# Layer 2 of six of nine token blocks in pairs, with seven block products in place of eight

## The chip, the core and the metric

The kernel runs on one core of one Trainium2 chip. The metric is device time in microseconds (us) of one execution. TensorE (PE) multiplies, VectorE (DVE) and ScalarE (ACT) work elementwise, GpSimd (POOL) and SyncE (SP) issue DMAs. Each engine takes its instructions strictly in its own order and waits on semaphores for the others.

## The reference, cut to what matters

An attention with pooled keys feeds two feed-forward layers of the same shape. A token block is 512 rows; there are nine.

```python
attn_out = _attn_ref(q, k, v)                  # 8 heads of 64: x is 4608 x 512
h = x @ w_in                                   # layer 1: 512 -> 2048
g = P(h) / (Q(h) + 1e-6)                       # rational function, elementwise
x = g @ w_out                                  # 2048 -> 512
h = np.maximum(x @ w_in2, 0.0)                 # layer 2: 512 -> 2048
out = h * h @ w_out2                           # 2048 -> 512
```

## The kernel before

Every fp32 operand of a large product is held as two parts, HI (rounded to fp32r) and LO (the rest), and each product is three passes: HI*HI, HI*LO, LO*HI. The hidden width of 2048 is cut into 16 tiles of 128. A **slot** is one hidden tile of one token block: `mm1` makes h in one PSUM bank with 12 matmuls of 512 columns (4 row blocks times 3 passes), ACT and DVE turn h into g (`first`, `second`), and three slots later (LAG) `mm2` adds the tile's part of the output into four PSUM banks y0 to y3, again with 12 matmuls. So a slot is 24 matmuls, and 9 blocks, 2 layers and 16 tiles make 288 slots.

The blocks go in groups (SBS: 2, 2, 2 and 3 blocks). A group runs four phases of 8 tiles: two for layer 1, two for layer 2. A phase's eight weight tiles (1 MB each: w_in and w_out rows, HI and LO) stay in eight buffers `w` while all blocks of the group use them; after the first group they come from a copy in DRAM, `ws`. After a phase, ACT or DVE take the four banks out to `ya`, `yb` or `t` (`evac`). The attention of later blocks (36 chunks of 128 tokens) lies between the slots, as do the decoding of the weights in the first group and the DMA transposes and pooled sums of the attention.

The order on each engine is not the order of the code. The code records operations with costs, and the class `Plan` lists them on each engine by due time; `Plan.emit` writes them out in that order. All compute is recorded in helper functions, so the profile gives one line (L390) for nearly every row, and rows are told apart by tile names: `h<-x,w` is mm1, `y<-w,g` mm2 of layer 1 or `y<-g,w` the other operand order, `sc`, `xp`, `e`, `mx`, `q`, `a`, `at` belong to the attention, `kp`, `vp` to the pooled sums.

Of the kernel before, what the change touches and what calls it, by code (L numbers as in the profile page):

```python
# [22 lines left out]
POOL = 8  # L23
# [16 lines left out]
SBS = [[0, 1], [2, 3], [4, 5], [6, 7, 8]]  # L40
# [6 lines left out]
NORM_DVE = {0, 2, 3, 5}  # L47
# [5 lines left out]
TWOS = {c for sb in SBS for c in range(max(NF, CPB * sb[0]), CPB * sb[-1] + CPB - 1, 2)}  # L53
# [5 lines left out]
X_DMA = ()  # L59
SB1_START, SB1_STEP = 39, 3  # L60
# [51 lines left out]
class PlannedTile(View):  # L112
    def __init__(self, pool, bufs, shape, dtype, name):
        super().__init__(self)
        self.pool, self.bufs, self.shape, self.dtype, self.name = pool, bufs, shape, dtype, name
        self.writes, self.reads, self.made, self.psum = [], [], None, False

    def real_tile(self):
        if self.made is None:
            self.made = self.pool.tile(self.shape, self.dtype, name=self.name)  # L120
        return self.made
# [9 lines left out]
class Plan:  # L131
# [15 lines left out]
    def tile(self, pool, bufs, shape, dtype, name):  # L147
        t = PlannedTile(pool, bufs, shape, dtype, name)
        tiles = self.tags.setdefault((id(pool), name), [])
        tiles.append(t)  # L150
        return t
# [245 lines left out]
def fused_kernel(  # L397
# [13 lines left out]
    out: bass.AP,  # L411
):
# [3 lines left out]
    class Pool:  # L416
# [4 lines left out]
        def tile(self, shape, dtype, name):  # L421
            t = plan.tile(self.pool, self.bufs, shape, dtype, name)
            t.psum = self.psum
            return t
# [5 lines left out]
    px = Pool("px", 4)  # L430
    pw = Pool("pw", FH)
    PS = bass.MemoryType.PSUM
    ps_h = Pool("ps_h", 2, space=PS)
# [4 lines left out]
    scratch = {}  # L438
    sb_of = {j: sb for sb in SBS for j in sb}

# [38 lines left out]


# [34 lines left out]
    wt, raw_t = {}, {}  # L515
# [15 lines left out]

    def w_decode(ph, f):
# [13 lines left out]
        t = pw.tile([128, 2, 2 * TB], F32R, "w")  # L546
# [10 lines left out]
        wt[f] = t  # L557
# [29 lines left out]
    def kv_first():  # L587


        k, v = (px.tile([128, 2, 4, TB], F32, "x").rearrange("p a b c -> p (a b c)") for _ in range(2))  # L590
        kr = k[:, 0:H // 2 * S].rearrange("p (g k r) -> p g k r", g=H // 2, r=POOL)
        vr = [v[0:min(128, S - 128 * c), TB * c:TB * (c + 1)] for c in range(5)]
        for b, t in enumerate((k, v)):
            kp_t[b] = t[:, 6 * TB:6 * TB + H // 2 * SP].rearrange("p (g k) -> p g k", g=H // 2)
            vp_t[b] = t[0:SP, 7 * TB:8 * TB]

        def k_sum(b):
            plan.ahead = K_AHEAD if b == 0 else 0.0
            for g in range(H // 2):
                load(128 * S * 4, kr[:, g], kf[b, g].rearrange("p (k r) -> p k r", r=POOL))  # L600
                dve(S, "tensor_reduce", out=kp_t[b][:, g], in_=kr[:, g], axis=AX.X, op=ALU.add)
# [4 lines left out]
        def v_sum(b):  # L606
            plan.ahead = AHEAD if b == 0 else 0.0
            ps = ps_h.tile([128, TB], F32, "h")[0:SP]
# [43 lines left out]
    def q_first(c):  # L652

        if c == 0:
            t = f32(pw.tile([128, 2, 2 * TB], F32R, "w")).rearrange("p a n -> p (a n)")
            q_in[0] = t.rearrange("p (c h t) -> p c h t", c=4, h=4)
# [189 lines left out]
    def x_out(c):  # L846
        ps = x_ps.pop(c)
        j, o = divmod(c, CPB)
        if o == 0:
            xt[j] = px.tile([128, 2, 4, TB], F32R, "x")  # L850
        x = xt[j][:, :, :, o * CH:(o + 1) * CH]
        sc = 2.0 ** -A_SHIFT / POOL
        act(TB, AF.Copy, out=x[:, HI], in_=ps, scale=sc)
        stt(TB, x[:, LO], ps, sc, f32(x[:, HI]), ALU.mult, ALU.subtract)
# [6 lines left out]
    def mm1(i, u, f):  # L861
        ps = ps_h.tile([128, TB], F32, "h")
        w, x = wt[f], xt[u[0]]
        started[i] = pe(2.72, [
            dict(
                out=ps, lhsT=w[:, a, kc * 128:(kc + 1) * 128], rhs=x[:, b, kc, :],
# [6 lines left out]
    def mm2(i, u, f, ds=range(4)):  # L873
        g, w = gt[i], wt[f][:, :, TB:2 * TB]
        if f == 0:
            yps[u] = [ps_y.tile([128, TB], F32, f"y{d}") for d in range(4)]
        for d in ds:
            dd = slice(d * 128, (d + 1) * 128)
            mm = []
            for n, (a, b) in enumerate(PASSES):  # L880
                l, r = (w[:, a, dd], g[:, b]) if u[1] < 2 else (g[:, a, dd], w[:, b])
                mm.append(dict(
                    out=yps[u][d], lhsT=l, rhs=r,
                    start=(f == 0 and n == 0), stop=(f == FH - 1 and n == 2),
                ))
            pe(0.68, mm)

    def last_block(u, tiles):


        t, _ = ysb.pop(u[0])
        for d in range(4):
            for i in tiles:
                mm2(i, u, i % FH, (d,))
            for h in range(2):
                hh = slice(h * TB // 2, (h + 1) * TB // 2)
                tt(TB // 2, t[d][:, hh], yps[u][d][:, hh], t[d][:, hh], ALU.add)
                r0 = u[0] * TB + d * 128
                load(2 ** 17, out[r0:r0 + 128, hh], t[d][:, hh])

    def evac(u):
        j, ph = u
        y = yps.pop(u)
        if ph % 2 == 0:
            k = sb_of[j].index(j)
            if k < 2:
                t = p1.tile([128, 4, TB], F32, "y" + "ab"[k])
                ysb[j] = [t[:, d] for d in range(4)], t
            else:
                t = [p2.tile([128, 2, H, CH], BF16, "t") for _ in range(2)]  # L910
                ysb[j] = [f32(t[d // 2].rearrange("p a h t -> p a (h t)")[:, d % 2]) for d in range(4)], None
            for d in range(4):
                act(TB, AF.Copy, out=ysb[j][0][d], in_=y[d])
            return
        t, whole = ysb.pop(j)
        for d in range(4):
            tt(TB, t[d], y[d], t[d], ALU.add)
            if ph == 1:
                act(TB, AF.Copy, out=xt[j][:, HI, d], in_=t[d])
                if j in X_DMA:  # L920
                    act(TB, AF.Copy, out=xt[j][:, LO, d], in_=t[d], scale=-1.0)
            else:
                r0 = j * TB + d * 128
                load(2 ** 18, out[r0:r0 + 128, :], t[d])
        if ph == 1 and j in X_DMA:
            load_add(2 ** 20, f32(xt[j][:, LO]), whole)
        elif ph == 1:
            for d in range(4):
                tt(TB, xt[j][:, LO, d], t[d], f32(xt[j][:, HI, d]), ALU.subtract)

    def first(i, u):

        h = hps[i]
        s = p2.tile([128, TB], F32, "s")
        if u[1] >= 2:
# [3 lines left out]
        v = p2.tile([128, TB], F32, "v")  # L939
        t = p2.tile([128, TB], F32, "p")  # L940
# [8 lines left out]
        mid[i] = (s, v, t)  # L949

    def second(i, u):
        hps.pop(i)
        w = p1.tile([128, TB], F32, "w")
        g = p3.tile([128, 2, TB], F32R, "g")
        gt[i] = g
        if u[1] >= 2:
            (r,) = mid.pop(i)
            act(TB, AF.Square, out=g[:, HI], in_=r)
# [3 lines left out]
        q, r0, p = mid.pop(i)  # L962
# [7 lines left out]
    units = []  # L970
    for sb in SBS:
        for ph in range(4):
            units += [(j, ph) for j in sb]
    N = len(units) * FH
    nxt = {}
    for n, u in enumerate(units[:-1]):
        if units[n + 1][1] != u[1]:
            nxt[u] = units[n + 1][1]


# [147 lines left out]
```

## Time and profile before

| what | value |
|---|---|
| three runs | 1687.99, 1689.12, 1690.29 us, median 1689.12 |
| profiled execution | span 1686.5 us from first to last instruction; the profile gives no time of its own beside the span |
| PE busy | 1664.1 us, 99% |
| VectorE, ScalarE busy | 1126.8 us (67%), 1110.3 us (66%) |
| DMA | 237.8 MB, q1 (SP) busy 39.4% of 16 engines, q0 (POOL) 7.9% |

The median lies 2.6 us above the profiled span: start and end of an execution that the span leaves out. A share of busy time is a mean over stages; the windows in the rows below tell them apart. Matmuls are pipelined: one row of a matmul of 512 columns reads 389 ns, but the next begins long before that, so the pace is read from the starts of groups.

### The profile page before, as it was taken

Reading aid. Unit: us, or ns where it says so; the run is one execution under the profiler, and the core shown is the slowest. Engines: PE = TensorE matmul, PEld = TensorE weight load, DVE = VectorE, ACT = ScalarE, POOL = GpSimd, SP = SyncE. Lnnn points to the kernel's source line nnn. Section 1 sums busy time; section 2 is a strip of 40 time slices with the busy share of each in tenths; the row PEclk is TensorE's granted clock in tenths of the full one; section 3 lists DMA queues with packets and bytes.
Section 4 is the critical chain, followed back from the end, with each engine's and each line's share of the span. In section 5 each row is a group of like instructions: output and inputs, shape, how many; then the busy total and the mean of one; then the engine's idle time right before and its main releaser. Section 6 shows DMA issues by size and latency. Waiting matters only on the chain.

```text
span 1686.5 us, 23265 instructions
## 1 busy us (share of the span) xinstructions
PE 1664.1 (99%) x8764; PEld 1362.6 (81%) x8764; DVE 1126.8 (67%) x1794; ACT 1110.3 (66%) x2260; POOL 77.6 (5%) x95
## 2 busy tenths in 40 slices
PE   7899999999999999999999999999999999999998
PEld 4687888888888888888888888888888888888887
DVE  7999996664888963344899953447988998111112
ACT  6989778896566767765666877667766665333332
POOL 0001100110000111100001111000000000000000
PEclk9999999999999999999999999999999999999999
DMA  8358678978523565836145767646104005004001
GB/s 276 111 206 234 175 242 274 257 204 253 173 100 127 130 200 118 228 76 200 49 164 133 188 169 158 176 125 188 26 26 175 1 1 200 1 1 175 25 26 50
DMA packets 106976, 237.81 MB, mean 141 GB/s; under 512 B 63632, under 2 KB 65520, under 8 KB 86384
## 3 DMA queue, kind: packets, MB, share of 16 engines
q1 hardware_dynamic: 96352, 216.17, 39.4%
q0 software_dynamic: 10512, 20.16, 7.9%
q8 instruction: 69, 1.13, 0.3%
q14 instruction: 43, 0.35, 0.1%
HBM read 176.69 MB, written 42.99 MB: 130 GB/s over the span
## 4 chain that ended last, share of the span: by engine, by line
PE 92%; DVE 5%; ACT 2%; DMA 1%; issue 0%; SPq 0%; DVEq 0%; ACTq 0%
PE h L390 44%; PE y L390 44%; PE xp L390 2%; PE sc L390 1%; DVE w L390 1%; DVE p L390 1%; DVE g L390 1%; ACT v L390 1%; DMA ya<-wa 0%; DVE s L390 0%; ACT w L390 0%; ACT yb L390 0%; DVE t L390 0%; DMA w<-qf 0%; DVE x L390 0%
## 5 line engine op out<-in xcount | busy, mean ns | idle before, releaser
L390 PE MATMUL h<-x,w 128*128 128x512 f32 x3456 | 834.8, 390 | 3.7 <-DVE p L390 3.4
L390 PEld LDWEIGHTS h<-x,w 128*128 128x128 f32 x3456 | 645.9, 188 | 141.7 <-DVE p L390 3.0
L390 PE MATMUL y<-g,w 128*128 128x512 f32 x1728 | 418.0, 390 | 0.7 <-DVE g L390 0.7
L390 PE MATMUL y<-w,g 128*128 128x512 f32 x1728 | 417.2, 390 | 0.0
L390 PEld LDWEIGHTS y<-g,w 128*128 128x128 f32 x1728 | 323.2, 188 | 68.4 <-DVE g L390 1.2
L390 PEld LDWEIGHTS y<-w,g 128*128 128x128 f32 x1728 | 323.1, 188 | 67.6 <-DVE g L390 0.4
L390 DVE TENSOR_TENSOR g<-w,g 128x512 fp32r<-128x512 f32 x144 | 99.5, 691 | 314.9 <-ACT g L390 305.8
L390 ACT ACTIVATE s<-h 128x512 f32<-128x512 f32 x288 | 171.7, 596 | 209.2 <-PE h L390 193.1
L390 ACT ACTIVATE v<-s,ln_bias 128x512 f32<-128x512 f32 x144 | 104.6, 726 | 145.4 <-DVE s L390 144.7
L390 ACT ACTIVATE g<-s 128x512 fp32r<-128x512 f32 x144 | 91.0, 632 | 95.2 <-PE y L390 94.8
L390 ACT ACTIVATE p<-h,a_sb 128x512 f32<-128x512 f32 x144 | 111.9, 777 | 42.7 <-PE h L390 41.2
L390 DVE SCALAR_TENSOR_TENSOR g<-p,a_sb,v 128x512 fp32r<-128x512 f32 x144 | 107.7, 748 | 29.0 <-ACT v L390 26.4
L390 DVE TENSOR_TENSOR p<-p,h 128x512 f32<-128x512 f32 x144 | 98.0, 680 | 21.5 <-ACT p L390 9.4
L390 DVE SCALAR_TENSOR_TENSOR w<-p,a_sb,w 128x512 f32<-128x512 f32 x144 | 107.5, 747 | 2.0
L390 DVE SCALAR_TENSOR_TENSOR p<-p,a_sb,h 128x512 f32<-128x512 f32 x144 | 106.6, 740 | 2.0 <-ACT v L390 0.8
L390 DVE SCALAR_TENSOR_TENSOR s<-s,b_abs,v 128x512 f32<-128x512 f32 x144 | 107.1, 744 | 0.0
L390 ACT ACTIVATE v<-h,b_sb 128x512 f32<-128x512 f32 x144 | 99.3, 690 | 10.2 <-DVE p L390 5.6
L390 ACT ACTIVATE v<-v,ex_bias 128x512 f32<-128x512 f32 x144 | 104.1, 723 | 2.8
L390 DVE SCALAR_TENSOR_TENSOR w<-s,g 128x512 f32<-128x512 f32 x144 | 99.1, 688 | 3.3
L390 DVE TENSOR_TENSOR g<-w,v 128x512 fp32r<-128x512 f32 x144 | 98.7, 685 | 1.5
L390 ACT ACTIVATE w<-s 128x512 f32<-128x512 f32 x144 | 91.0, 632 | 9.6 <-DVE g L390 6.8
L390 ACT ACTIVATE e<-e,sm 128x72 f32<-128x72 f32 x256 | 69.9, 349 | 1.4 <-DVE sm L390 1.1
(111 smaller groups left out, 1058.0 us busy)
## 6 DMA issues: line engine op xcount, KB each, us to landing
w<-ws SPq DMA_DIRECT2D x96, 1024.0 KB, 5.5
ws<-w SPq DMA_DIRECT2D x32, 1024.0 KB, 5.5
q<-qt SPq DMA_DIRECT2D x27, 512.0 KB, 3.8
kp<-kt POOLq DMA_DIRECT2D x42, 288.0 KB, 4.6
wraw<-wb SPq DMA_DIRECT2D x8, 1024.0 KB, 7.2
wraw<-wa SPq DMA_DIRECT2D x7, 1024.0 KB, 6.4
yb<-wa SPq DMA_DIRECT2D x6, 1024.0 KB
vp<-vt POOLq DMA_DIRECT2D x42, 144.0 KB, 4.1
```

What stands on the lines that cost most here:

```text
L390: made = fn(**{k: v.real() if isinstance(v, View) else v for k, v in kw.items()})
```

## The change

Blocks 0 and 1 keep the four phases. Blocks 2 to 8 then run layer 1 one block at a time over all 16 tiles (`("one", j)`), with the weight tiles fetched again for each block. Block 2 runs layer 2 in the old way (`("two", 2)`). Blocks 3 and 4, 5 and 6, 7 and 8 run layer 2 as **pairs**. In a pair the two halves of each operand make 2 x 2 block matrices: the two token blocks are the columns on one side, and w_in and w_out are cut in two on both sides. Strassen's scheme (the form with shared sums) takes seven block products p1 to p7 where eight stood. A block product is a **group** of 6 matmuls of 512 columns; a pair has 8 double tiles times 7 groups for h, and 4 rounds times 7 products times 2 halves for y: 112 groups.

The operands of the products are sums of the halves. Those of the weights (`w_sums`, 8 double tiles times two parts) are made once on DVE and ACT and stored in DRAM (`wf`); those of the token blocks (`pair_forms`, tiles `xf`) are made at the start of a pair; those of g (`prepare`, tiles `gf`) at each round. The sums of products are not made on PE alone: a group is added on top of the bank of an earlier one (chains p1, p6, p7, p4 in one bank and p5, p3 in another), and after each group ACT or DVE read the partial sum out of the open bank into `ga`, `gb`, `gc`, `gd` (for h) or `acc` (for y). The next group in that bank waits for this read.

The weight loads of a pair are 72 pieces of 0.25 or 0.5 MB (`wi`, `wo`). The x of blocks 3 to 8 goes to DRAM when its attention is done (`xd`, 256 KB pieces with rows of 512 bytes) and comes back before the block. All chunks from 8 on scale their attention weights on DVE (`NORM_DVE`). The last half-tile evacuation (`last_block`) is gone. Results of the pairs are stored transposed.

The core of the diff:

```diff
-SBS = [[0, 1], [2, 3], [4, 5], [6, 7, 8]]
+FIRST_TWO = [0, 1]
+PLAIN = 3
+PAIRS = [(3, 4), (5, 6), (7, 8)]
+SEQ = [
+    ("one", 2), ("one", 3), ("two", 2), ("one", 4), ("pair", (3, 4)), ("one", 5), ("one", 6),
+    ("pair", (5, 6)), ("one", 7), ("one", 8), ("pair", (7, 8)),
+]
+PAIR_SLOTS, PAIR_STEPS = 28, 4
+NFT = DFF // 128
...
+NORM_DVE = {0, 2, 3, 5} | set(range(8, NCHUNK))
...
+SUM_AT = {n: 49 + 4 * (n - 4) for n in range(4, 8)} | {n: 98 + 2 * n for n in range(4)}
+CHUNK_AT = (
+    {8 + n: 38 + 3 * n for n in range(8)} | {16 + n: 92 + 3 * n for n in range(6)}
+    | {22 + n: 128 + 4 * n for n in range(6)} | {28 + n: 190 + 3 * n for n in range(8)}
+)
...
+        s2, s1, s3, s4 = (s[:, i // 2, i % 2 * h:(i % 2 + 1) * h] for i in S_PLACES[part])
+        tt(h, s1, a21, a22, ALU.add)
+        tt(h, s2, s1, a11, ALU.subtract)
+        tt(h, s3, a11, a21, ALU.subtract)
+        tt(h, s4, a12, s2, ALU.subtract)
+        flat = s.rearrange("p a c -> p (a c)")
+        hi, lo = (o[:, i].rearrange("p a c -> p (a c)") for i in (HI, LO))
+        act(2 * TB, AF.Copy, out=hi, in_=flat)
+        tt(2 * TB, lo, flat, f32(hi), ALU.subtract)
+        sums_of[n, part] = pd.tile([128, 2, 4, h], F32, f"wf{n}_{part}")
+        load(WB, sums_of[n, part], f32(o), STORE_EARLY)
...
+    def pair_forms(pair):
+        a, b = pair
+        (b11, b21), (b12, b22) = x2.pop(a), x2.pop(b)
+        made = {}
+
+        def form(p, x):
+            t = x_tile([128, 2, 2, TB], "xf", FORM_TAGS[pair][p])
+            split(t[:, HI], t[:, LO], x, 2 * TB)
+            made[p] = t
+
+        n = 2 * TB
+        form("p1", b11)
+        form("p2", b21)
+        tt(n, b11, b12, b11, ALU.subtract)
+        form("p5", b11)
+        tt(n, b12, b22, b12, ALU.subtract)
+        form("p3", b22)
+        tt(n, b22, b22, b11, ALU.subtract)
+        form("p6", b22)
+        form("p7", b12)
+        tt(n, b21, b21, b22, ALU.subtract)
+        form("p4", b21)
+        forms[pair] = made
...
+    Y_FORMS = (("p1", "p2"), ("p5", "p3"), ("p6", "p7"), ("p4",))
+    Y_ORDER = [p for ps in Y_FORMS for p in ps]
+    H_ORDER = ("p1", "p2", "p6", "p5", "p7", "p3", "p4")
+    HEAD_ORDER = ("p1", "p2", "p5", "p6", "p3", "p7", "p4")
...
+        def wi(n):
+            t = w_tile([128, 2, 4 * HT], "wi", 6 * (n % 2))
+            load(WB / 2, f32(t[:, :, 0:TB]), src(n, 0, slice(0, TB)), FETCH_EARLY)
+            load(WB / 2, f32(t[:, :, TB:2 * TB]), sums(n, 0, 0), FETCH_EARLY)
+            u = w_tile([128, 2, 4 * HT], "wi", 6 * (n % 2) + 1)
+            load(WB / 2, f32(u[:, :, 0:TB]), sums(n, 0, 2), FETCH_EARLY)
+            load(WB / 4, f32(u[:, :, TB:TB + HT]), src(n, 1, slice(HT, TB)), FETCH_EARLY)
+            at = {p: (t, m) for m, p in enumerate(FIRST_H)} | {p: (u, m) for m, p in enumerate(LAST_H)}
+            return {p: t[:, :, m * HT:(m + 1) * HT] for p, (t, m) in at.items()}
...
+            def step(p):
+                if not w:
+                    w.update(wi(n))
+                a, b, c, d = (t[:, q] for t in blocks_of(r))
+                if p == "p1":
+                    bank["x"] = ps_h.tile([128, TB], F32, "h", f"h{n if n < 2 else 0}")
+                if p in ("p2", "p5"):
+                    bank["z"] = ps_y.tile([128, TB], F32, "hz", "y3" if n == 1 else "y0")
+                x = bank["z" if p in ("p2", "p5", "p3") else "x"]
+                op = pe(1.36, [
+                    dict(
+                        out=x, lhsT=w[p][:, i, kt * 128:(kt + 1) * 128], rhs=forms[pair][p][:, j, kt],
+                        start=(p in ("p1", "p2", "p5") and m == kt == 0), stop=(m == 2 and kt == 1),
+                        skip_group_check=True,
+                    )
+                    for m, (i, j) in enumerate(PASSES) for kt in range(2)
+                ])
+                t = dict(p1=a, p2=a, p6=b, p5=d, p7=d, p3=b, p4=c)[p]
+                if p in ("p1", "p5", "p6"):
+                    act(TB, AF.Copy, out=t, in_=x)
+                elif p == "p4":
+                    sq(t, x)
+                else:
+                    tt(TB, t, x, t, ALU.add)
+                    sq(t, t)
+                return op
+
+            return [lambda p=p: step(p) for p in (HEAD_ORDER if n < 2 else H_ORDER)]
...
+            def prepare(k):
+                p = Y_ORDER[k]
+                a, b, c, d = blocks_of(r)
+                n = 2 * TB
+                if p == "p5":
+                    tt(n, a, b, a, ALU.subtract)
+                elif p == "p6":
+                    tt(n, d, d, a, ALU.subtract)
+                elif p == "p4":
+                    tt(n, c, c, d, ALU.subtract)
+                x = dict(p1=a, p2=c, p5=a, p3=d, p6=d, p7=b, p4=c)[p]
+                t = p1.tile([128, 2, 2, TB], F32R, "gf", "y" + "ab"[k % 2])
+                split(t[:, HI], t[:, LO], x, n)
+                if p == "p3":
+                    tt(n, b, d, b, ALU.subtract)
+                ring[p] = t
+                if k % 2 == 0:
+                    ws.update(wo(r, k // 2))
+
+            def group(k, i):
+                p = Y_ORDER[k]
+                if i == 0:
+                    prepare(k)
+                if not acc:
+                    acc.extend(f32(w_tile([128, 4, TB], "acc", 4 + m)) for m in range(2))
+                if p == "p1":
+                    bank["x", i] = ps_y.tile([128, TB], F32, "yx", f"y{1 + i}")
+                if p in ("p2", "p5"):
+                    bank["z", i] = (ps_h if i else ps_y).tile([128, TB], F32, "yz", "h1" if i else "y3")
+                x = bank["z" if p in ("p2", "p5", "p3") else "x", i]
+                op = pe(1.36, [
+                    dict(
+                        out=x, lhsT=ws[p, q][:, a, i * 128:(i + 1) * 128], rhs=ring[p][:, b, q],
+                        start=(p in ("p1", "p2", "p5") and m == q == 0), stop=(m == 2 and q == 1),
+                        skip_group_check=True,
+                    )
+                    for m, (a, b) in enumerate(PASSES) for q in range(2)
+                ])
+                o = dict(p1=0, p2=0, p6=1, p3=1, p4=2, p5=3, p7=3)[p]
+                t = acc[i][:, o]
+                if r == 0 and p in ("p1", "p5", "p3", "p4"):
+                    act(TB, AF.Copy, out=t, in_=x)
+                else:
+                    tt(TB, t, x, t, ALU.add)
+                if r == FH // 2 - 1 and p in ("p2", "p6", "p7", "p4"):
+                    r0 = (2 * (o // 2) + i) * 128
+                    load(2 ** 18, outt[(ta, tb)[o % 2], r0:r0 + 128, :], t)
+                return op
+
+            return [lambda k=k, i=i: group(k, i) for k in range(7) for i in range(2)]
...
+        hs = [h_steps(n) for n in range(FH)]
+        steps = [h for two in zip(hs[0], hs[1]) for h in two]
+        for r in range(1, FH // 2):
+            for h, y in zip(hs[2 * r] + hs[2 * r + 1], y_steps(r - 1)):
+                steps += [h, y]
+        return steps + y_steps(FH // 2 - 1)
```

The engine orders show it at three places. First PE near the end of layer 2 of block 8 (h the hidden tile, y0 to y3 the output banks). Before:

```order
L390 MATMUL h_14954<-x_11370,w_14288 128x512 x12
L390 MATMUL y0_14934<-w_14185,g_14891 128x512 x3
L390 MATMUL y1_14940<-w_14185,g_14891 128x512 x3
L390 MATMUL y2_14946<-w_14185,g_14891 128x512 x3
L390 MATMUL y3_14950<-w_14185,g_14891 128x512 x3
L390 MATMUL h_14986<-x_11370,w_14327 128x512 x12
```

And in the last pair now (h and hz are the two banks of a hidden double tile, yx and yz those of y, two of each):

```order
L409 MATMUL h_14691<-xf_14049,wi_14493 128x512 x6
L409 MATMUL hz_14751<-xf_13993,wi_14493 128x512 x6
L409 MATMUL yz_14761<-gf_14675,wo_14655 128x512 x6
L409 MATMUL h_14691<-xf_14023,wi_14553 128x512 x6
L409 MATMUL yz_14782<-gf_14746,wo_14687 128x512 x6
L409 MATMUL hz_14751<-xf_14012,wi_14553 128x512 x6
L409 MATMUL yz_14800<-gf_14746,wo_14687 128x512 x6
L409 MATMUL h_14691<-xf_14067,wi_14553 128x512 x6
L409 MATMUL yz_14782<-gf_14776,wo_14687 128x512 x6
L409 MATMUL yz_14800<-gf_14776,wo_14687 128x512 x6
```

A bank such as h_14691 now comes back every three or four groups with other work between, where before it held one sum of 12 matmuls and was read once.

Second, DVE at the end of the program (t is the output tile before; acc the output, gf the LO part of a form of g, ga to gd its sums). Before:

```order
L390 TENSOR_TENSOR g<-w,g 128x512 x6
L390 TENSOR_TENSOR t<-y_14934,t 128x256 x2
L390 TENSOR_TENSOR t<-y_14940,t 128x256 x2
L390 TENSOR_TENSOR t<-y_14946,t 128x256 x2
L390 TENSOR_TENSOR t<-y_14950,t 128x256 x2
```

And now, the first twelve rows from the last hidden sum on (eight more of the same kinds follow):

```order
L409 TENSOR_TENSOR gb<-hz,gb 128x512
L409 TENSOR_TENSOR gf<-gc,gf 128x1024
L409 TENSOR_TENSOR acc<-yx,acc 128x512
L409 TENSOR_TENSOR ga<-gb,ga 128x1024
L409 TENSOR_TENSOR acc<-yx,acc 128x512
L409 TENSOR_TENSOR acc<-yz,acc 128x512
L409 TENSOR_TENSOR gb<-gd,gb 128x1024
L409 TENSOR_TENSOR gf<-ga,gf 128x1024
L409 TENSOR_TENSOR acc<-yz,acc 128x512
L409 TENSOR_TENSOR gf<-gd,gf 128x1024
L409 TENSOR_TENSOR gd<-gd,ga 128x1024
L409 TENSOR_TENSOR acc<-yz,acc 128x512
```

PE's own end is now `yx<-gf,wo` x12, `yz<-gf,wo` x36 and `yx<-gf,wo` x36, 14 groups with no h group between them, and each product needs a form from this list.

Third, the SP queue in layer 2. Before, one of the 1 MB fetches for each slot:

```order
L390 DMA w<-ws_0_3473 128x2048
L390 DMA w<-ws_1_3588 128x2048
L390 DMA w<-ws_2_3631 128x2048
L390 DMA w<-ws_3_3796 128x2048
L390 DMA w<-ws_4_3872 128x2048
```

And in the last pair now:

```order
L409 DMA wo_14411<-wf2_1_6390 128x2x512
L409 DMA wo_14411<-wf3_1_6547 128x2x512
L409 DMA wi_14423<-wf5_0_3835 128x2x512
L409 DMA wi_14423<-ws3_3_3515 128x2x256
L409 DMA wi_14493<-ws3_4_3520 128x2x512
L409 DMA wi_14493<-wf6_0_4081 128x2x512
L409 DMA wo_14505<-wf2_1_6390 128x2x512
L409 DMA wo_14505<-wf3_1_6547 128x2x512
```

The same stretch of PE work is now fed by two to four pieces where one transfer stood.

## Rows read from the trace of the kernel before

**Rows 1.** Page: span and busy time of PE.

```profile
span 1686.5 us, 23265 instructions
...
PE 1664.1 (99%) x8764; PEld 1362.6 (81%) x8764; DVE 1126.8 (67%) x1794; ACT 1110.3 (66%) x2260; POOL 77.6 (5%) x95
```

**Rows 2.** Windows: us, busy of PE, PEld, DVE, ACT, POOL; granted clock; DMA.

```profile
0.00:40.00 40.00, 28.61 (x180) 17.06 (x180) 29.89 (x60) 23.52 (x69) 1.25 (x8) 0.91 0.85 289
40.00:80.00 40.00, 35.40 (x261) 27.44 (x260) 39.90 (x71) 38.85 (x94) 0.00 (x0) 1.00 0.34 119
...
200.00:300.00 100.00, 99.99 (x471) 82.06 (x470) 82.18 (x122) 78.29 (x145) 7.24 (x8) 1.00 0.76 238
300.00:400.00 100.00, 100.00 (x661) 81.99 (x660) 65.81 (x104) 85.94 (x215) 8.92 (x10) 1.00 0.82 221
...
1300.00:1400.00 100.00, 100.00 (x443) 82.84 (x442) 92.34 (x141) 62.66 (x99) 0.00 (x0) 1.00 0.08 29
...
1500.00:1600.00 100.00, 100.00 (x443) 82.83 (x442) 13.18 (x19) 38.03 (x63) 0.00 (x0) 1.00 0.24 84
```

**Rows 3.** All waits of PE: waiting engine and tile, releaser, us, times, longest.

```profile
PE y L390 <- DMA w<-qf: 8.0, 1, 8.0
PE h L390 <- DVE p L390: 3.4, 3, 1.6
```

**Rows 4.** Timeline of layer 2, last group: start us, length us, engine, tile.

```profile
1502.50 2.88 PE L390 MATMUL y<-w,g 128*128 128x512 f32 x12
1502.70 0.60 ACT L390 ACTIVATE s<-h 128x512 f32<-128x512 f32 x1 [2.09 <-PE h L390]
...
1505.22 2.88 PE L390 MATMUL h<-x,w 128*128 128x512 f32 x12
1505.42 0.63 ACT L390 ACTIVATE g<-s 128x512 fp32r<-128x512 f32 x1 [1.46 <-PE y L390]
1506.08 0.69 DVE L390 TENSOR_TENSOR g<-w,g 128x512 fp32r<-128x512 f32 x1 [4.75 <-ACT g L390]
```

**Rows 5.** Costliest groups by form: total busy us, mean ns of one.

```profile
L390 DVE TENSOR_TENSOR w<-wraw,w 128x1024 fp32r<-128x1024 f32 x12 | 14.6, 1221 | 4.2 <-ACT w L390 4.2
...
L390 ACT ACTIVATE w<-wraw 128x1024 fp32r<-128x1024 f32 x12 | 13.9, 1156 | 2.7 <-DVE wraw L390 1.8 <-PE y L390 0.9
```

**Rows 6.** Timeline of DVE in layer 1, back to back.

```profile
174.26 0.68 DVE L390 TENSOR_TENSOR p<-p,h 128x512 f32<-128x512 f32 x1
174.85 1.22 DVE L390 TENSOR_TENSOR w<-wraw,w 128x1024 fp32r<-128x1024 f32 x1
175.99 0.69 DVE L390 SCALAR_TENSOR_TENSOR w<-s,g 128x512 f32<-128x512 f32 x1
```

**Rows 7.** Timeline of the end.

```profile
1675.67 6.51 PE L390 MATMUL y<-w,g 128*128 128x512 f32 x28
...
1679.31 4.52 SPq L390 DMA_DIRECT2D out_dram<-t  x8
1681.54 1.43 DVE L390 TENSOR_TENSOR t<-y,t 128x256 f32<-128x256 f32 x4 [1.28 <-PE y L390]
```

**Rows 8.** Landing of the eight 256 KB stores of the last group.

```profile
DMA to landing us min/median/max: 2.1/2.1/2.1
```

**Rows 9.** Short windows: two transposes; fetches; stores of 256 KB; of 128 KB.

```profile
1180.00:1185.00 5.00, 5.00 (x40) 4.04 (x40) 4.97 (x11) 3.28 (x6) 0.00 (x0) 1.00 0.51 105
...
1390.00:1400.00 10.00, 10.00 (x46) 8.29 (x45) 9.97 (x17) 5.87 (x10) 0.00 (x0) 1.00 0.53 188
...
1647.00:1649.00 2.00, 2.00 (x11) 1.65 (x10) 1.22 (x2) 0.49 (x1) 0.00 (x0) 1.00 1.01 379
...
1680.00:1682.00 2.00, 2.00 (x10) 1.48 (x8) 0.71 (x3) 0.00 (x0) 0.00 (x0) 1.00 0.78 257
```

**Rows 10.** DMA of the whole span: the queue of POOL.

```profile
q0 software_dynamic: 10512, 20.16, 7.9%
```

**Rows 11.** DMA issues after 1200 us: fetches, KB each, us to landing.

```profile
w<-ws SPq DMA_DIRECT2D x24, 1024.0 KB, 4.8
```

More of the change, by code (lines that the diff above doesn't have):

```diff
@@ L871, in mm1, with mm2 @@
         hps[i] = ps
-    def mm2(i, u, f, ds=range(4)):
-        g, w = gt[i], wt[f][:, :, TB:2 * TB]
-        if f == 0:
+    def mm2(i, u, layer, wf, first, last):
+        g, w = gt.pop(i), wf[:, :, TB:2 * TB]
+        if first:
             yps[u] = [ps_y.tile([128, TB], F32, f"y{d}") for d in range(4)]
-        for d in ds:
+            if u[0] == "two":
+                ysb[u[1]] = p1.tile([128, 4, TB], F32, "yo", "w4")
+        for d in range(4):
             dd = slice(d * 128, (d + 1) * 128)
@@ L880, in mm2 @@
             for n, (a, b) in enumerate(PASSES):
-                l, r = (w[:, a, dd], g[:, b]) if u[1] < 2 else (g[:, a, dd], w[:, b])
+                l, r = (w[:, a, dd], g[:, b]) if layer == 0 else (g[:, a, dd], w[:, b])
                 mm.append(dict(
                     out=yps[u][d], lhsT=l, rhs=r,
-                    start=(f == 0 and n == 0), stop=(f == FH - 1 and n == 2),
+                    start=(first and n == 0), stop=(last and n == 2),
                 ))
             pe(0.68, mm)
[L888 to L899, printed above, removed]
     def evac(u):
@@ L904, in evac @@
         if ph % 2 == 0:
[L905 to L911, printed above, removed]
+            t = p1.tile([128, 4, TB], F32, "y", "y" + "ab"[j])
+            ysb[j] = t
             for d in range(4):
[L913 removed]
+                act(TB, AF.Copy, out=t[:, d], in_=y[d])
@@ L933, in first, with evac_two @@
+    def evac_two(j):
+        y, t = yps.pop(("two", j)), ysb.pop(j)
+        for d in range(4):
+            act(TB, AF.Copy, out=t[:, d], in_=y[d])
+            r0 = j * TB + d * 128
+            load(2 ** 18, out[r0:r0 + 128, :], t[:, d])
+    def first(i, layer):
         h = hps[i]
-        s = p2.tile([128, TB], F32, "s")
-        if u[1] >= 2:
+        sv = p2.tile([128, 2, TB], F32, "sv")
+        s = sv[:, 0]
+        if layer:
             act(TB, AF.Relu, out=s, in_=h)
@@ L1048, in fused_kernel, with tile_slot @@
             at(t + f, "t", w_decode, ph, f)
-    for n, u in enumerate(units):
-        if u in nxt and n >= 4 * len(SBS[0]) - 1:
-            for f in range(FH):
-                at(n * FH + f + LAG, "x", w_fetch, nxt[u], f)
+    slots = [("half", (j, ph), f) for ph in range(4) for j in FIRST_TWO for f in range(FH)]
+    begins = {}
+    for what, x in SEQ:
+        if what == "pair" and slots[-1][0] == "one":
+            slots += [("gap", None, None)] * LAG
+        begins[what, x] = len(slots)
+        slots += [(what, x, f) for f in range(PAIR_SLOTS if what == "pair" else NFT)]
+    N = len(slots)
+    steps = {pair: pair_steps(pair) for pair in PAIRS}
+    for n, t in SUM_AT.items():
+        for part in range(2):
+            at(t + 2 * part if n >= 4 else t, "x", w_sums, n, part, "w1" if n < 4 and part else "x3")
+    for j in range(PLAIN, NB):
+        at(begins["one", j] - 2, "x", x_fetch, j)
+    FORMS_AT = {
+        pair: begins["pair", pair] - 1 for pair in PAIRS
+    }
+    for pair, t in FORMS_AT.items():
+        at(t, "x", pair_forms, pair)
+    wf_t = {}
+    def tile_slot(i):
+        what, x, f = slots[i]
+        if what == "half":
+            j, ph = x
+            return j, ph // 2, wt_of[ph, f], x, f == 0, f == FH - 1, evac
+        layer = int(what == "two")
+        if i not in wf_t:
+            wf_t[i] = w_fetch(x, layer, f)
+        done = evac_two if layer else evac_one
+        return x, layer, wf_t[i], (what, x), f == 0, f == NFT - 1, lambda u: done(u[1])
     setup()
```

291 lines of the change are left out of this document (186 added, 105 removed).

## The prediction

> **What bounds the kernel now.** I read the page first: the span is 1686.5 us and PE is busy for 1664.1 of them [rows 1]. A busy PE need not be a PE at its pace, so next the windows: from 200 us on PE is busy all of each window at clock 1.00, which is the 2.4 GHz level, whether VectorE has 92.34 us of work in 100 (layer 1, at 1300) or 13.18 (layer 2, at 1500) [rows 2]. Third, the waits of PE: over the whole execution the list names 8.0 us for the first data and 3.4 us for VectorE, and little else [rows 3]. Last, the timeline of layer 2 gives the pace: 12 matmuls start at 1502.50 and the next 12 at 1505.22, so 2.72 us for 12, 0.227 us each, 5.44 us for a slot [rows 4]. PE sets the end; a matmul less is 0.227 us less, as long as the others keep up.
>
> **What is removed.** A pair of blocks cost 2 x 16 slots x 24 = 768 matmuls of 512 columns in layer 2. Now it is 112 groups of 6, that is 672. Three pairs save 288, and at the pace of [rows 4] that is 288 x 2.72 / 12 = **65.3 us**. Nothing else leaves PE, and what stays has the same shape, so the pace should stay.
>
> **What is added, and what hides it.**
>
> *VectorE and ScalarE inside a pair.* In the order of the last pair VectorE has 72 instructions of 512 columns and 53 of 1024. One of 1024 reads 1221 ns [rows 5], but overlaps the next: back to back they start 0.60 us apart (174.26 to 174.85) and 1.14 us apart (174.85 to 175.99) [rows 6]. That makes 72 x 0.60 + 53 x 1.14 = 104 us, under a PE time of 672 x 0.227 = 152 us. The first two pairs also carry six to eight chunks of attention, about 6 us of VectorE each by the same pitches, so up to 151 us, while PE has the products of these chunks on top of its 152. Layer 1 already runs with 92% of VectorE and PE loses nothing [rows 2]. So neither engine becomes the bound; what can cost is the order of the work. In the body of a pair three other groups (4.1 us) lie between two uses of a bank. Reading a bank ends 0.8 us after PE could go on (PE free at 1502.50, ScalarE 1502.70 + 0.60) [rows 4], so 3.3 us of other work may stand ahead of the read, nearly three long VectorE instructions. In the last pair I take nothing for this. In the two pairs with attention I take three or four times one instruction of 1.14 us too many, 4 us each, **+8 us**. No row shows a bank read while its sum goes on, so the bounds are 0 and 0.3 us for each of the 336 groups (100 us); I stay near 0 because the 92% of layer 1 is the nearest case.
>
> *The start of a pair.* With the last sums of y0 and y1, PE still has 12 matmuls and three groups that need nothing new, 6.8 us. The next product (p5) needs two reads by ScalarE (done at 1.4 us with hops of 0.2 us, as between 1502.50 and 1502.70), a difference on VectorE (2.8), its HI on ScalarE (4.2), and its bank must have been read by VectorE, which by its order first makes the LO (5.6) and the next difference (6.8): 7.5, so PE waits some 0.8 us; the second p5 waits another 0.7 us behind the next LO, and two later groups 0.2 us each. Together 2 us, three times **+6 us**; bounds 0 (PE finds other work) and 5 us each.
>
> *The end.* After the last hidden group PE has 14 groups of y, 19.0 us, with only one group between two uses of a bank. VectorE's list there is 15 instructions of 512 and 10 of 1024 columns, 20.4 us, and it idles some 3 us because three times it needs the HI of a form that ScalarE (1156 ns [rows 5]) can start only when a buffer is free. So PE ends some 4.8 us later than its own work. Behind PE's end nothing is won: before, PE ended at 1675.67 + 6.51 = 1682.2 and the span at 1686.5, 4.3 us [rows 7]; now it is one read of 0.69 us, an issue and a store of 256 KB that lands in 2.1 us [rows 8], about the same. **+5 us**, bounds 2 and 9.
>
> *DMA.* Weights are now fetched for each block: 112 MB for layer 1 of blocks 2 to 8, 16 MB for layer 2 of block 2 and 28 MB for each pair, 212 where 96 stood, with 16 MB more of stored sums and 24 of x out and in. One fetch in a slot keeps the engines busy at 0.53 for 188 GB/s, so 350 GB/s while busy; stores of 256 KB pieces (2 KB rows) 379 at 1.01 and of 128 KB (1 KB rows) 257 at 0.78, 330 [rows 9]. Small pieces thus cost the engines little more than large ones. In a pair 28 MB in 152 us is 0.55 of the engines. The tightest place is the four layers from block 2 to block 4 with the sums of weights: the order has there 95 MB by SP (100e6 bytes, 285 us at 350 GB/s), 12 transposes at 1.3 us (two: 0.51 of 5 us [rows 9]) and 35 accumulating loads by POOL at 1.5 us (7.9% of 1686.5 us over 87 [rows 10]), 353 us, while PE has 64 slots, 348 us, and some 20 to 30 us of attention. A fetch that takes 4.8 us alone [rows 11] will take longer there; layer 1 has eight buffers, up to four slots ahead, but layer 2 of block 2 has five. I take **+5 us**. Bounds: 0, since at 200 to 400 us the engines ran at 0.76 and 0.82 and PE lost nothing [rows 2]; and 50 us, if they reach only that window's 221 / 0.82 = 270 GB/s.
>
> The Trainium skill's page "DMA: Bandwidth & Descriptors", section Bandwidth, speaks against the change: it wants 1 MiB in one transfer and gives a smaller one a fixed 2 us. By it, if nothing overlapped, 72 pieces and 28 MB would take 144 + 67 = 211 us for a pair (an estimate from its formula), 59 us over PE's 152; the trace does not agree, its eight small stores ran at 330 GB/s of engine time.
>
> *The sums of weights* are 16 times two instructions of 512, four of 256 (0.36 us [rows 7]) and one of 1024 columns, 3.8 us, 60 us of VectorE in all; 28 chunks more scale on VectorE (0.7 us each). Half of the sums fall at 270 to 350 us, where VectorE was busy for 66 to 82 of 100 us [rows 2], and half beside layer 2 of block 2, where it has little else. Hidden, but late sums hold weight buffers: **+2 us**, bounds 0 and 10.
>
> The clock gets no term: at 40 to 80 us PE was busy for 35.40 of 40 and the granted clock was 1.00; it was below that (0.91) only in the first 40 us [rows 2], and the waits above are shorter.
>
> **The sum.** -65.3 + 8 + 6 + 5 + 5 + 2 = -39.3, so a span of 1647.2 us. The runs lie 2.6 us above the profiled span (median 1689.12), which gives **1650 us**.
>
> **Rivals.** *Banks in pairs:* the wait for a read takes the place of the removed products. For it speaks that the two engines sit in a loop of reads, forms and products in a fixed order, against it that VectorE has a third of a pair free. At 0.05 us more for each of 336 groups it is 1667 us, at 0.1 us 1683; from 0.12 us the gain is gone. *DMA in blocks 2 to 4* (the other side): if the engines reach 270 GB/s there, 95 MB take 369 us, 437 with the rest, some 65 us more than PE; less the 5 that I have taken, 1710 us. It decides from about 290 GB/s down. Against it: 350 while busy in the short windows. *Small transfers don't overlap:* from 2.1 us for 0.25 MB and 4.8 for 1 MB [rows 8, 11] a transfer has 1.2 us of its own and 3.6 us per MB, so a pair takes 72 x 1.2 + 28 x 3.6 = 187 us where PE needs 152, three times 35: 1755 us. Against it, eight stores of 128 KB were issued within 4.52 us with the engines at 0.78 [rows 7, 9]. The page of the Trainium skill named above has such a rule. *Nothing waits:* PE finds other work at each place, 1624 us.
>
> **Chances.** Forecast, 1634 to 1664 us: 0.62. Below 1634: 0.08. Banks, 1664 to 1684: 0.16. Between there and 1700, from several of them: 0.04. DMA in blocks 2 to 4: 0.07. Small transfers: 0.03. The range 1634 to 1684 holds 0.78. A measurement of this kernel can tell about 0.2% (3.4 us) from no change: faster 0.86, same 0.03, slower 0.11.
>
> **What would show it.** Right: PE busy without gaps through layer 1; starts of 6 matmuls 1.36 us apart in the body of a pair; waits of PE of about 2 us at three places and 5 in the last 24 us; 20 to 30 us of PE waits in all, most of them for VectorE. Wrong: waits for DMA of several us from block 2 to block 4, or of wi and wo in the pairs; a granted clock below 1.00 in a pair; waits at nearly every group. Then the sum fails at that term.

## The result, and the profile after

The changed kernel takes 1660.87 us (median of 4, 1659.67 to 1662.32), the kernel before 1689.01 in the same comparison: ratio 0.983, 95% interval 0.9816 to 0.9844. The forecast was 1650 in a range of 1634 to 1684. So the direction and the range held, and 10.9 us of the forecast gain did not come.

The page of the profile after: the span and TensorE's row (busy us, share, instructions), which answer to [rows 1].

```profile
span 1657.9 us, 23637 instructions
PE 1624.2 (98%) x8476; PEld 1309.3 (79%) x8476; DVE 1411.3 (85%) x2135; ACT 1134.0 (68%) x2105; POOL 77.8 (5%) x95
```

The span fell by 28.6 us; PE's busy time fell by 39.9, and the time in which PE has no row rose by only 11.3 (22.4 to 33.7). 288 matmuls fewer should have taken 65.3 from the busy time. So the first place to look is not a wait but PE's pace.

The timeline of PE in layer 1 of block 8 (start, length, what, count), to be laid beside [rows 4]:

```profile
1421.91 2.90 PE L409 MATMUL h<-x,w 128*128 128x512 f32 x12
1424.65 2.96 PE L409 MATMUL y<-g,w 128*128 128x512 f32 x12
1427.44 2.90 PE L409 MATMUL h<-x,w 128*128 128x512 f32 x12
1430.18 2.95 PE L409 MATMUL y<-g,w 128*128 128x512 f32 x12
1432.97 2.90 PE L409 MATMUL h<-x,w 128*128 128x512 f32 x12
```

From y to the next h it is 2.79 us, where 12 matmuls took 2.72; a slot is 5.53 us, where it was 5.44. No wait stands in these rows. The body of a pair keeps the old pace, 6 matmuls in 1.36 us:

```profile
1540.54 1.52 PE L409 MATMUL h<-xf,wi 128*128 128x512 f32 x6
1541.90 1.52 PE L409 MATMUL yx<-gf,wo 128*128 128x512 f32 x6
1543.26 1.52 PE L409 MATMUL hz<-xf,wi 128*128 128x512 f32 x6
```

The waits of PE over the whole execution (us, times, longest), the answer to [rows 3]:

```profile
PE y L409 <- DMA q<-qf: 7.6, 1, 7.6
PE h L409 <- DVE pq L409: 3.9, 6, 1.4
...
PE yz L409 <- DVE acc L409: 2.1, 2, 1.1
PE h L409 <- DMA w<-ws: 2.0, 1, 2.0
PE hz L409 <- ACT gd L409: 1.6, 1, 1.6
PE yz L409 <- DVE gf L409: 1.4, 1, 1.4
```

To place the loss I took the start of every matmul from the trace and split the time from the first to the last (1673.8 us before, 1645.9 after) into parts:

```
us                                                    before   after   difference
512-column matmuls x 0.22667 (6931, 6643)             1571.05 1505.77    -65.3
starts up to 0.39 us apart, over 0.22667: plain slots    11.1    24.3    +13.2
the same, groups of the pairs                               0     6.1     +6.1
starts over 0.39 us apart, less 0.22667: first 110 us    12.1    14.1     +2.0
the same, from 110 us on                                  2.7    17.6    +14.9
small matmuls of the attention                           76.8    78.1     +1.3
```

The differences sum to -27.8, against -28.6 of the span. The products gave exactly the forecast 65.3. All waits and small delays but those of the plain slots make 24.3 us, for the 26 of the forecast. What the forecast did not have at all is the second line: in the plain slots (those outside the pairs) each start is a little later than its pace would have it.

### The profile page after: what moved, and what is told of

Read it like the earlier page. It is cut to its first block, busy times and chain, and to the rows that moved or that the text cites. A ratio compares the mean times of both kernels' runs of the same rounds, so it can differ in the third digit from the quotient of the medians.

```text
span 1657.9 us, 23637 instructions
## 1 busy us (share of the span) xinstructions
PE 1624.2 (98%) x8476; PEld 1309.3 (79%) x8476; DVE 1411.3 (85%) x2135; ACT 1134.0 (68%) x2105; POOL 77.8 (5%) x95
## 4 chain that ended last, share of the span: by engine, by line
PE 76%; DVE 15%; DMA 4%; ACT 3%; issue 2%; SPq 0%; DVEq 0%; ACTq 0%
PE h L409 33%; PE y L409 26%; PE yx L409 6%; DVE pq L409 5%; PE hz L409 5%; PE yz L409 4%; DVE g L409 2%; DVE sv L409 1%; PE xp L409 1%; DMA vp<-vt 1%; PE sc L409 1%; DVE t L409 1%; DMA xd<-xo 1%; ACT sv L409 1%; DVE acc L409 1%
## 5 line engine op out<-in xcount | busy, mean ns | idle before, releaser
L409 PE MATMUL h<-x,w 128*128 128x512 f32 x2304 | 559.3, 392 | 8.3 <-DVE pq L409 3.9
L409 PEld LDWEIGHTS h<-x,w 128*128 128x128 f32 x2304 | 431.6, 188 | 107.0 <-DVE pq L409 6.1
L409 ACT ACTIVATE sv<-h 128x512 f32<-128x512 f32 x192 | 114.0, 594 | 76.3 <-PE h L409 59.5
L409 PE MATMUL h<-xf,wi 128*128 128x512 f32 x576 | 145.7, 391 | 0.3 <-DVE gd L409 0.3
L409 PE MATMUL y<-w,g 128*128 128x512 f32 x576 | 143.4, 397 | 0.1
L409 PE MATMUL yx<-gf,wo 128*128 128x512 f32 x576 | 142.6, 390 | 0.4 <-DVE acc L409 0.4
L409 ACT ACTIVATE pq<-h,a_sb 128x512 f32<-128x512 f32 x144 | 111.9, 777 | 29.1 <-PE h L409 19.9
L409 PEld LDWEIGHTS y<-w,g 128*128 128x128 f32 x576 | 107.4, 188 | 25.5 <-DVE g L409 0.5
L409 ACT ACTIVATE sv<-h,b_sb 128x512 f32<-128x512 f32 x144 | 98.9, 687 | 28.6 <-DVE g L409 16.5
L409 PE MATMUL yz<-gf,wo 128*128 128x512 f32 x432 | 108.8, 392 | 4.0 <-DVE acc L409 2.1
L409 PE MATMUL hz<-xf,wi 128*128 128x512 f32 x432 | 110.0, 392 | 2.2 <-ACT gd L409 1.6
L409 DVE TENSOR_TENSOR pq<-pq,h 128x512 f32<-128x512 f32 x144 | 98.2, 682 | 10.2 <-ACT pq L409 5.4
```

The source lines that it names most:

```text
L409: made = fn(**{k: v.real() if isinstance(v, View) else v for k, v in kw.items()})
```

## The experiments

### A slower pace without a wait

The matmuls of a y group in layer 1 are the same in both kernels; what differs in them is where their tiles lie. In the built programs the byte addresses in a partition of SBUF, taken modulo 256, are:

```
                         g (stationary or moving)   w, x    gf, wo, xf, wi
kernel before                     224                224         -
changed kernel                    224                 96        96
```

So the groups with equal places run at full pace, and those of g with w, whose places are 128 bytes apart, do not. Four kernels, and later a fifth, with the order of instructions unchanged on every engine tested it. The first moves g in the changed kernel:

```diff
+    p3 = Pool("p3", 3)
     p1 = Pool("p1", 1)
     p2 = Pool("p2", 2)
-    p3 = Pool("p3", 3)
```

> The changed kernel with the pool of the g tiles placed ahead of the pool of weights and x, so that g starts at byte 352 of a 2048-byte unit as x, w, gf and wo do (it stood at 2016). Order and work are the same. Theory A (TensorE's pace depends on how the moving and the stationary tile lie to each other in SBUF): y groups of the plain slots start their matmuls 226.7 ns apart, not 232.9, h groups 227 and not 228.1; 2107 starts x 6.2 ns + 2116 x 1.1 ns, about 15 us, so a span of about 1643 and a time of 1644 to 1648 us. Rival B (the fetch of weights for every slot and DMA traffic slow TensorE): 232.9 ns and 1661 us as before this edit. Rival C (waits of each group for semaphores): 1661 us too.

The others take the kernel before and push x and w away from g by unused bytes (384, 1024 and 128; later 256):

```diff
     p3 = Pool("p3", 3)
+    Pool("pp", 1).pool.tile([128, 96], F32, name="pad")
     px = Pool("px", 4)
```

> The kernel before with 384 unused bytes behind the g tiles, so that x and w move from byte 2016 to byte 352 of a 2048-byte unit and g stays at 2016, as they lie in the changed kernel. Order and work are the same. Theory A: y groups go from 226.7 to 232.9 ns, h groups to 228.1: 3456 x 6.2 ns + 3456 x 1.2 ns = 26 us more, 1715 us. Rivals B and C (fetches, waits): nothing in them has changed, 1689 us and 226.7 ns.

> The kernel before with 1024 unused bytes behind the g tiles (x, w and g 1024 bytes apart in a unit of 2048). If only an equal place in a unit of 2048 bytes is fast: 232.9 ns in the y groups and about 1715 us. If what counts repeats every 256, 512 or 1024 bytes: 226.7 ns and 1689 us.

> The kernel before with 128 unused bytes behind the g tiles. If what counts repeats every 128 bytes or less, 226.7 ns and 1689 us, but then the 384 bytes of the other edit would be fast too; by theory A 232.9 ns and about 1715 us, or something between, if the slowing grows with the distance.

> The kernel before with 256 unused bytes behind the g tiles. 1024 were fast, 128 and 384 slow. If what counts repeats every 256 bytes: 226.7 ns in the y groups, 1689 us. If it repeats only every 512 or 1024: 232.9 ns and about 1714 us.

The mean from start to start inside groups, from 200 us on, starts over 0.30 us apart left out:

```
                               h<-x,w   y<-g,w   y<-w,g  ns      time us
kernel before                   226.9    226.8    227.0          1689
before, 128 unused bytes        228.8    232.8    232.9          1712.8 (one)
before, 256                     226.9    226.8    226.9          1689.3 (one)
before, 384                     228.8    232.9    232.9          1715.2 (4)
before, 1024                    226.9    226.8    227.0          1689.3 (one)
changed kernel                  228.3    232.9    233.0          1660.9
changed kernel, g first         227.1    226.9    227.3          1654.8 (5)
```

With 384 bytes the ratio to the kernel before is 1.015 (1.0131 to 1.0169): 384 unused bytes cost 25 us, as expected, in a kernel with no new fetch and no new wait. Its timeline has the rows of the changed kernel, here from the same place in time:

```profile
1421.89 2.90 PE L390 MATMUL h<-x,w 128*128 128x512 f32 x12
1424.62 2.96 PE L390 MATMUL y<-g,w 128*128 128x512 f32 x12
1427.42 2.90 PE L390 MATMUL h<-x,w 128*128 128x512 f32 x12
```

The changed kernel with g first shows 2.72 again, in both kinds of groups:

```profile
1423.01 2.88 PE L409 MATMUL y<-g,w 128*128 128x512 f32 x12
1425.72 2.88 PE L409 MATMUL h<-x,w 128*128 128x512 f32 x12
1428.44 2.88 PE L409 MATMUL y<-g,w 128*128 128x512 f32 x12
```

So theory A holds, and rivals B (fetches) and C (waits) fall for the pace. 256 and 1024 bytes are fast, 128 and 384 slow: as far as these distances show, what counts repeats every 256 bytes. Distances other than 128 within the 256 were not tried.

The time of the kernel with g first was not as expected, though: its profiled execution took 1645.9 us, the other four 1653.6 to 1658.3 (ratio 0.98, 0.9784 to 0.9817). It was run again beside the changed kernel:

> The changed kernel itself, beside the runs below on the same chip: 1661 us (1659 to 1663), y groups of the plain slots at 232.9 ns.

> The kernel with the g tiles first once more, because its five times went from 1646 to 1658 us where the kernel before stayed within 4 us. If the pace is all: 1645 to 1648 us, and the longer times belonged to that chip. If a faster TensorE now meets the weights that come just in time: again a spread of 8 us and more, some 1646 to 1658 us, and waits for w or wf tiles in the trace of a long one.

On one chip the changed kernel took 1661.35 us (ratio 0.9839, 0.9825 to 0.9852) and with g first 1651.17 (0.977, 0.9756 to 0.9783), with a spread of 3.5 us. That lies between the two expectations: the spread is gone, but the median is above 1648. So the alignment is worth 10.2 us in the median. In the trace the plain slots' starts lose 24.3 - 10.1 = 14.2 us of excess; of the remaining 4, starts over 0.39 us apart give back 2.0 (17.6 to 19.6 from 110 us on), and the rest may lie within the spread. The spread of the first chip stays unexplained; no trace of one of its long executions exists.

### Waits from block 2 to block 4

The waits that the forecast gave to DMA lie in layer 2 of block 2 and layer 1 of block 4. On top of the kernel with g first, layer 1 of blocks 3 and 4 fetched half the bytes (LO passes read HI):

```diff
+HALF = {(3, 0), (4, 0)}
...
+        if (j, layer) in HALF:
+            load(WB / 2, f32(t[:, HI]), src[:, HI], FETCH_EARLY)
+        else:
+            load(WB, f32(t), src, FETCH_EARLY)
```

> The kernel with the g tiles first, and blocks 3 and 4 in layer 1 fetch only the HI half of their weight tiles (0.5 MB for 1 MB, 16 MB less in all); their LO passes read HI instead, so the numbers of these blocks are left out, and the products are as many as before. Theory (the waits from block 2 to block 4, 6 to 7 us there, and the spread come from the rate of the DMA engines): these waits fall below 3 us, the spread below 4 us, and the time is 1640 to 1645 us. Rival (they come from the order of SyncE's queue, which stands behind issues that wait for other engines): waits and spread stay as they are, 1646 to 1658 us.

This gave 1644.49 us (0.9734, 0.9721 to 0.9747) and few waits there, as the theory of the rate wanted, though the spread did not fall below 4 us (it is 4.7). But the planner (the class `Plan`) takes sizes into account, and all engines had another order. So the two were parted, bytes without order and order without bytes, by giving the planner WB for the half fetch, or WB / 2 for the whole one:

> As the run with half fetches in blocks 3 and 4 (layer 1 of these blocks reads HI for LO, so their numbers are left out), but the planner is told the full size, so that every engine has the order of the kernel with the g tiles first, word for word; only the bytes differ. Theory (the rate of the DMA engines): the waits of layer 2 of block 2 and layer 1 of block 4 fall from 7.6 to below 3 us and the time to 1643 to 1646 us. Rival (the order of the queues, which the planner changed in the run before): the waits stay at 6 to 8 us and the time at 1650 to 1653 us.

> The other half of the same question: full fetches, nothing left out, in the order that the planner made for the half fetches. Theory (rate): the waits from block 2 to block 4 come back, 1650 us or more. Rival (order): 1643 to 1647 us, and a version that is faster than the kernel with the g tiles first.

Starts over 0.39 us apart, less 0.227, in us:

```
                                   layer 2, block 2   layer 1, block 4   time us
changed kernel, two profiles           4.0, 2.0           2.9, 3.8       1661
g first                                4.3                3.3            1651.2
half bytes, planner's own order        0.2                1.4            1644.5
half bytes, order of g first           1.9                3.3            1651.4
full bytes, order of the half bytes    0.7               10.6            1656.4
scaling on ScalarE                     0.2                0.0            1649.7
scaling on ScalarE, 16 to 35           1.8                0.0            1649.5
```

In the same order, halving the bytes of block 4 changes nothing for PE, though the DMA share falls. The windows of 700 to 800 us (busy us of PE, weight loads, VectorE, ScalarE, GpSimd; granted clock, DMA share, GB/s), first with full and then with half bytes:

```profile
700.00:800.00 100.00, 97.43 (x461) 77.88 (x461) 85.67 (x130) 64.77 (x100) 9.48 (x11) 1.00 0.94 283
```

```profile
700.00:800.00 100.00, 97.42 (x461) 78.16 (x461) 86.26 (x131) 64.66 (x100) 9.48 (x11) 1.00 0.74 202
```

So in this order the rate of the engines is not what block 4 waits for, and the theory falls there; its waits are for `pq`, that is VectorE (2.2 us in three with half bytes). VectorE is not behind with its work there, though. In the changed kernel it was idle for 6.58 us just before, until ScalarE had made `sv`, and ScalarE for 9.72 us, until PE had made h:

```profile
753.63 0.60 ACT L409 ACTIVATE sv<-h 128x512 f32<-128x512 f32 x1 [9.72 <-PE h L409]
754.84 0.75 DVE L409 SCALAR_TENSOR_TENSOR sv<-sv,b_abs 128x512 f32<-128x512 f32 x1 [6.58 <-ACT sv L409]
757.04 3.02 PE L409 MATMUL h<-x,w 128*128 128x512 f32 x12 [1.35 <-DVE pq L409]
```

The three wait for each other in a circle. The half fetch could not test layer 2 of block 2, whose own tiles stayed whole; its one wait for a weight tile (2.0 us in the changed kernel) may be rate or queue. Whether the row there reads about 4 or about 2 us is mostly the clock: in the profiles with 4.0 and 4.3 seven starts of 0.43 us and more follow the wait, in those with 2.0 and 1.9 none.

In the other order, full bytes bring a 5.7 us wait, and the granted clock is 0.93 from 740 to 790 us. ScalarE and VectorE there (waits from 765 to 785 us) show how a DMA reaches PE: ScalarE waits for the load of a pooled sum of keys, VectorE behind it for ScalarE, and PE for VectorE:

```profile
ACT k L410 <- DMA kp<-kt: 10.0, 1, 10.0
DVE kp L410 <- ACT k L410: 9.7, 1, 9.7
```

In that order the bytes decide, so the half-bytes run mixed two causes: 1644.5 needs both.

If block 4 waits for VectorE's work, less of it should help. In the kernel with g first, with full fetches, the scaling of the attention weights went back to ScalarE, once for all chunks from 8 on, once for 16 to 35:

```diff
-NORM_DVE = {0, 2, 3, 5} | set(range(8, NCHUNK))
+NORM_DVE = {0, 2, 3, 5}
```

> The kernel with the g tiles first, and the scaling of the attention weights of chunks 8 to 35 back on ScalarE, as before the change. If VectorE has the time for it, as the prediction took it: no difference within 3 us. If VectorE is what TensorE waits for in layer 1 (it is 92 to 97% busy there): 5 us or more faster. If ScalarE's reads of banks come later by it: slower by some us.

> The kernel with the g tiles first, and the scaling on ScalarE for chunks 16 to 35 alone (chunks 8 to 15 stay on VectorE). Theory (the waits in layer 1 of block 4 are for VectorE's attention work, not for DMA: with all chunks from 8 on ScalarE they were 0.2 us in place of 7.6): again below 2 us from block 2 to block 4, and 1645 to 1649 us, as long as the pairs keep the 9 us of waits they had. Rival (a moved order gives back elsewhere what it gains here, as the run with all chunks did in the pairs): 1649 to 1652 us.

The waits of block 4 are gone in both (0.0), with full fetches, so its 3 us did not need fewer bytes to go. But the planner gave every engine another order here too, so these two runs do not show whether less work on VectorE or the other order took them away; the circle of waits above speaks for the order. The window of 600 to 700 us, with the scaling on VectorE and then on ScalarE:

```profile
600.00:700.00 100.00, 97.67 (x590) 79.60 (x587) 70.28 (x134) 61.65 (x157) 0.90 (x1) 0.98 0.94 289
```

```profile
600.00:700.00 100.00, 99.99 (x622) 81.78 (x621) 69.02 (x136) 73.25 (x204) 0.00 (x0) 1.00 0.94 302
```

The time hardly moves: 1649.68 us (0.9764, 0.9746 to 0.9781) and 1649.46 (0.9758, 0.974 to 0.9777; six times, the profiled one its longest at 1656.8) beside 1651.17 (0.977). That is the rival of the last run. With all chunks the pairs' long starts rise from 9.3 us (2.6, 2.7 and 4.0) to 10.7 (3.8, 1.9 and 5.1), those of the first 64 slots from 6.9 to 8.4, and the small matmuls of the attention take 4.0 us more (80.9 to 84.9), with waits for VectorE's `sm`, `x` and `e` among them. These three versions beat both kernels, and can't be told from each other; moving g alone is the smallest edit.

## Why the prediction came out as it did

**Products, -65.3.** Right, to a tenth.

**"What stays has the same shape, so the pace should stay."** This is the step that failed. The shape stayed, the addresses did not: g moved behind the weights, 128 bytes off in 256, and the plain slots lost 13.2 us against the kernel before and 14.2 against the one with g first, more than the whole miss of 10.9. With g first the time is 1651.17, 1.2 over the forecast. Nothing in the rows of before could show it, since all operands lay alike there, but the built program of the changed kernel did. The Trainium skill's page "TensorE: Matmul & The Clock Gate", section "Step-by-step: what each phase is for", says that loading the next tile's weights takes no read bandwidth of SBUF from the running matmul. By it a weight load would not slow a running matmul wherever the tiles lie. The 232.9 ns, in both operand orders, hang on how the stationary and the moving tile lie to each other, which is at odds with that; but no run shows that it is the weight load that slows the matmul. What happens inside the chip stays open.

**The bodies of two pairs, +8.** About right. Long starts in the first pair and just behind it make 5.2 - 0.2 = 5.0 us, in the second 0.4; the small delays in the groups of all pairs are 6.1 us against nothing assumed for the last. In all 11.5 for 8. The rival of banks in pairs fell: beside these long starts 336 groups lost 0.02 us each.

**The starts, +6.** Too much: 0.2, 0.7 and 0.2 us, in all 1.1. PE found other work, as the lower bound had it.

**The end, +5.** Right in kind and place; 1.65, 1.26, 0.18 and 0.61, so 3.7 us, for VectorE's sums and forms:

```profile
1638.02 2.60 PE L409 MATMUL yz<-gf,wo 128*128 128x512 f32 x10 [1.37 <-DVE gf L409]
1641.70 3.30 PE L409 MATMUL yz<-gf,wo 128*128 128x512 f32 x12 [1.09 <-DVE acc L409]
...
1648.16 5.73 PE L409 MATMUL yx<-gf,wo 128*128 128x512 f32 x24 [0.45 <-DVE acc L409]
```

**DMA from block 2 to block 4, +5.** The size was near (4.0 + 2.9 = 6.9 us), the cause mostly not: 2.9 of it are the waits in the circle of PE, ScalarE and VectorE, which half the bytes in the same order left as they were, some 1.6 is clock, and about 2 are the one wait for a weight tile. The rival at 270 GB/s fell: over the four layers, from 421.5 to 803.9 us, the engines moved 285 GB/s at a share of 0.91, 313 while busy; the lowest of the four, layer 1 of block 4, has 276 at 0.93, 297.

```profile
421.50:803.90 382.40, 378.05 (x1910) 305.14 (x1909) 325.79 (x527) 244.59 (x448) 22.98 (x26) 1.00 0.91 285
```

**Small transfers.** They do overlap. In the last pair, from 1500 to 1600 us, PE is busy for 99.98 with the engines at 0.56:

```profile
1500.00:1600.00 100.00, 99.98 (x442) 82.42 (x441) 65.14 (x75) 62.25 (x95) 0.00 (x0) 1.00 0.56 184
```

In the same 100 us the queue of SP moved 18.35 MB (packets, MB, share of 16 engines) in 44 loads of 0.25 and 0.5 MB:

```profile
q1 hardware_dynamic: 11968, 18.35, 56.2%
```

The formula that the prediction weighed stands on the Trainium skill's page "DMA: Bandwidth & Descriptors" in the section "Anatomy of one DMA — SWDGE (gpsimd) path": about 2.0 us and the bytes at 436 GB/s for each transfer, of any size, fitted there to DMAs that GpSimd issues; the section Bandwidth has the rule of 1 MiB. If nothing overlapped, the 44 loads would take 88 + 42 = 130 us by it, an estimate, and they were issued within 100; the trace does not agree.

**Sums of weights, +2.** No wait of PE names them: hidden, as far as PE shows it.

**The list of waits.** It sums to 29.2 us, within the 20 to 30 foretold, but only 13.0 of them are for VectorE, so not most as foretold, and 7.6 are for the first data.

**"The clock gets no term."** Wrong by some 3 us, in two stretches. After the wait for a weight tile in layer 2 of block 2 a group of 12 takes 4.40 us:

```profile
646.96 2.26 PE L409 MATMUL y<-w,g 128*128 128x512 f32 x9
651.22 4.55 PE L409 MATMUL h<-x,w 128*128 128x512 f32 x12 [2.00 <-DMA w<-ws]
655.62 0.63 PE L409 MATMUL y<-w,g 128*128 128x512 f32 x2
```

and the window's granted clock is 0.52, the level of 1.2 GHz, before it is 1.00 again:

```profile
651.00:654.00 3.00, 2.78 (x7) 2.22 (x8) 2.53 (x4) 0.00 (x0) 0.00 (x0) 0.52 0.89 174
655.00:665.00 10.00, 10.00 (x65) 8.14 (x64) 6.58 (x14) 5.54 (x20) 0.00 (x0) 1.00 0.79 264
```

The other stretch lies near the start, where the kernel before had 1.00 from 40 to 80 us: after a wait of 1.58 us for g, 11 matmuls take 4.29 us.

```profile
60.65 4.36 PE L409 MATMUL y<-g,w 128*128 128x512 f32 x11 [1.58 <-DVE g L409]
60.00:65.00 5.00, 4.35 (x13) 3.22 (x14) 5.00 (x9) 4.58 (x13) 0.00 (x0) 0.66 0.66 226
```

**The sum of the waits, 24.3 for 26.** Near, but in part by luck. The bodies cost 11.5 for 8, the starts 1.1 for 6, the end 3.7 for 5, DMA from block 2 to block 4 6.9 for 5, the sums 0 for 2. No term stood for the 3.3 us of the first 110 us and of the small matmuls, nor for 0.5 in layer 1 of the last blocks; 2.7 us of the kernel before go off. The misses cancel.

## What to carry to other kernels

Before a term is taken for "the same work at the same pace", look up the addresses of the operands in both built programs: here 128 bytes between a matmul's two tiles, modulo 256, cost 2.7% of every such matmul and more than half of what all the new waits cost. A pace is compared by starts of groups, since busy shares and the list of waits showed nothing of it. And an experiment that changes sizes under a planner changes the order too: part the two, or the run answers neither question.

## What the runs showed of the hardware

- Matmuls of 512 columns whose moving and stationary tiles lie 128 bytes apart modulo 256 in SBUF start every 232.9 ns on average, and those with equal places every 226.7 to 227, whichever of the two tiles is the stationary one. The h groups that follow such a group are slower too, by some 1.5 ns in the mean, though their own tiles have equal places: in the changed kernel the first two starts of the 12 take 232.0 ns, the last but one 226.7.
- A clock at half level does not need a long wait. With half bytes in the order of g first, a matmul of the first pair starts 0.44 us late, and 0.7 us later seven starts of 0.43 us begin; the granted clock there is 0.50. After a start 1.6 us late in block 4 of the same run there was none.

```profile
857.90:861.00 3.10, 3.10 (x9) 2.40 (x8) 2.79 (x5) 3.07 (x6) 0.88 (x1) 0.50 1.06 300
```
